# Expert rows folded over features before they are stored, and a Fourier stage that folds over tokens only

## The chip, the cores and the metric

The kernel runs on one core of a Trainium2 chip. A core has five engines that run side by side: TensorE (PE, matrix multiplication), VectorE (DVE), ScalarE (ACT), GpSimd (POOL) and SyncE (SP), the last of which here only issues transfers. TensorE reads its operands from SBUF, the on-chip memory of 128 partitions, and writes to PSUM, from where VectorE and ScalarE take the results. Sixteen DMA engines move data between SBUF and the chip's main memory (DRAM in the names). The metric is the device time of one execution in microseconds (us).

## The reference

Three layers follow each other on arrays of 4 batches, 576 tokens and 512 features: attention that keeps the 32 largest scores of a row, a layer of eight experts in which each token goes to one expert, and a mixing layer. The change concerns the last two.

```python
# experts: e is the token's expert, p[e] its weight
h = np.maximum(x[b, s] @ w1[e], 0.0)
out[b, s] = p[e] * (h @ w2[e])
...
# mixing
X = np.fft.fft(x, axis=1)          # over 576 tokens
X = np.fft.fft(X, axis=2)          # over 512 features
mixed = np.real(X).astype(np.float32)
u = x + mixed
un = (u - mean) / np.sqrt(var + 1e-06)   # over features
ch = np.maximum(un @ w_ch1, 0.0) @ w_ch2
return (u + ch).astype(np.float32)
```

## The kernel before

A Fourier transform over n points is done with matrix products. Its real part needs, of a row, only the sums x[d] + x[512 - d] (which meet cosines) and the differences x[d] - x[512 - d] (which meet sines), and likewise over tokens s and 576 - s. Making these sums and differences is called folding here, and it halves the length of the products. All products are made of pairs of shorter numbers, a high part (names ending in h) and a low part (l) with value = high + low, in three matmuls: high by high, high by low, low by high.

**Expert stage** (lines 1066 to 1263). Tokens were sorted by expert, and expert r of 8 works on up to CAPS[r] = 512 to 256 rows. It goes through f = 0 to 7, one step each: `mm1` makes 128 hidden features (PSUM tile `m`), ScalarE and VectorE turn them into `hh` and `hl`, and `mm2`, two steps later, adds their share to the output of up to four tiles of 128 rows. Between them stand the splits of the next expert's weights (`whi`, `wlo`) and the preparation of its rows (`xh`, `xl`). After f = 7, `finish(r)` copies the output tiles from PSUM to `ysb` with the factor p, and `store(r)`, called in step f = 2 of the next expert, or at the end for the last, scatters each tile of `ysb` with an indirect transfer from GpSimd's queue (`to_rows`) to the array `xm_d` in DRAM. A batch has 2 x 289 rows there: first tokens 1 to 288 and 0, then tokens 575, 574, ... down to 289, so that a row and the one 289 rows on are the pair that is folded over tokens.

**Fourier stage** (lines 1325 to 1477), for b = 0 to 3. `load_x(b)` reads the two halves to `xa` and `xb` in pieces of 112, 112 and 65 rows. `fold` adds and subtracts them over tokens (`fe` on VectorE, `fo` on GpSimd) and then folds each over features (256 to 511 onto 256 to 1). `parts` makes the high and low parts `eh`, `el` (258 columns) and `oh`, `ol` (256 columns). `over_tokens(b, c)`, c = 0 to 4, has nine matmuls for each of five chunks of features, three for `eh` and two for `oh`; ScalarE and VectorE take each from PSUM as high and low parts `ch`, `cl` or `sh`, `sl`. `over_features(b, j)`, j = 0 to 2, has nine matmuls into `pc` and six into `pn`; ScalarE copies `pc` to `cs`, VectorE makes the difference and the sum with `pn` (`dd`), which are stored to `md_d`. Batch b + 1 is folded while batch b is multiplied; batch 0 has its own order in `first()`.

**Norm and mixing.** `norm(g)` takes 256 rows of the sum of `xm_d` (tile `ut`) and `md_d` (`md`): GpSimd adds them, VectorE makes the statistics (`bs`, `mv`), ScalarE the deviation (`sd`), VectorE the scaled rows (written to `md`), and TensorE transposes them (`lt`), from where `nxh` and `nxl` are taken. The first two groups are normalized in the last batch of the Fourier stage, by the list `nops`; the others in the mixing that follows, which is bound by its matmuls (`f`).

Every engine works through its own instructions in the order in which the code emits them; nothing is reordered at run time. SyncE's transfers are issued in order too, and one that waits holds back those behind it.

## Time and profile before

| | |
|---|---|
| median of 3 runs | 1267.19 us (1265.48 to 1268.96) |
| the profiled execution, its own time | 1266.99 us |
| its span, from the first to the last instruction | 1264.8 us |
| TensorE busy | 1194.6 us, 94% of the span |
| VectorE busy | 866.9 us, 69% |
| ScalarE busy | 676.3 us, 53% |
| GpSimd busy | 446.0 us, 35% |

A row of the profile names an engine, a line of the code, an operation, the tile that it writes and those that it reads, and a shape (partitions x elements). PEld is TensorE's loading of weights, which overlaps its matmuls (PE). An engine may start an instruction shortly before the one ahead of it ends. The granted clock of TensorE is given as a share of 2.4 GHz: 1.00 is that level and 0.50 the other, 1.2 GHz, and what lies between is a mean over a stretch at both.

### The profile page before, as it was taken

The page shows a single profiled execution, that of the slowest core. Times are in us where ns is not written, and L with a number is a line of the kernel's source. Part 1 is how long each engine was busy: PE and PEld are TensorE (multiplying, and loading weights), DVE is VectorE, ACT ScalarE, POOL GpSimd, SP SyncE. Part 2 cuts the span into 40 slices and gives each one's busy share as a digit, 9 for nine tenths or more (in the row PEclk, how much of TensorE's full clock was granted, in tenths as well). Part 3 has the DMA queues.
Part 4 walks back from the last instruction along what each step waited for, and adds up shares of the span by engine and source line. Part 5 has one row for each costly group of instructions (what it writes and reads, how often), then busy time and mean ns, then how long its engine had stood idle before and what let it go on. Part 6 is the DMA issues. An engine that isn't in the chain of part 4 may idle for free. (4 is left out here: it accounts for less than half of the span.)

```text
span 1264.8 us, 25173 instructions
## 1 busy us (share of the span) xinstructions
PE 1194.6 (94%) x8691; PEld 1086.4 (86%) x8691; DVE 866.9 (69%) x3559; ACT 676.3 (53%) x1426; POOL 446.0 (35%) x553
## 2 busy tenths in 40 slices
PE   6999999999998995999999995979999999999997
PEld 5999889998998994898888885869999999999996
DVE  7999999999998985475666665847744444443222
ACT  6999999999997992354444542323322222221110
POOL 3767776786875683011111102713200000000122
PEclk9999999999998998999999995989999999999998
DMA  5757634443451413876666756632310010100111
GB/s 113 193 149 199 143 86 116 115 103 86 124 131 44 138 49 109 259 270 216 213 228 218 231 174 191 194 115 80 102 67 34 34 67 20 49 1 1 50 51 51
DMA packets 125653, 152.25 MB, mean 120 GB/s; under 512 B 68175, under 2 KB 70471, under 8 KB 125402
## 3 DMA queue, kind: packets, MB, share of 16 engines
q1 hardware_dynamic: 120442, 133.34, 36.8%
q0 software_dynamic: 5072, 17.19, 3.8%
q8 instruction: 71, 1.16, 0.4%
q14 instruction: 68, 0.56, 0.1%
HBM read 92.05 MB, written 32.79 MB: 99 GB/s over the span
## 5 line engine op out<-in xcount | busy, mean ns | idle before, releaser
L474 POOL TENSOR_TENSOR y<-ss,g 128x576 f32<-128x576 f32 x144 | 185.3, 1287 | 116.2 <-ACT g L469 58.3
L448 DVE MAX8 cd<-ss 128x8 f32<-128x72 f32 x1152 | 218.2, 220 | 10.0 <-ACT ss L442 9.5
L1529 ACT ACTIVATE fhh<-f 128x256 fp32r<-128x256 f32 x144 | 55.1, 383 | 278.9 <-PE f L1525 274.4
L1530 DVE SCALAR_TENSOR_TENSOR fhl<-f,fhh 128x256 fp32r<-128x256 f32 x144 | 60.9, 423 | 205.9 <-ACT fhh L1529 205.8
L545 PE MATMUL u<-in_v,et 128*128 128x74 f32 (+1 forms) x1600 | 185.5, 265 | 4.9 <-DVE dv L704 2.5
L545 PEld LDWEIGHTS u<-in_v,et 128*128 128x128 f32 (+1 forms) x1600 | 177.5, 181 | 10.0 <-ACT st_x L552 4.0
L528 PE MATMUL tp<-ident,z 128*128 128x128 f32 x720 | 142.6, 284 | 4.8 <-DVE lo L355 4.6
L529 PE MATMUL tp<-huge_id,bb 128*128 128x128 bf16 x720 | 131.7, 220 | 0.3 <-ACT bb L507 0.3
L435 PE MATMUL acc<-kt,qp 128*128 128x288 f32 x640 | 125.2, 323 | 6.3 <-ACT ss L442 4.0
L1550 POOL DMA_INDIRECT out_dram<-ut,orow x18 | 17.5, 971 | 319.4 <-DVE ut L1546 317.5
L469 ACT ACTIVATE g<-ss,mt 128x576 bf16<-128x576 f32 x144 | 118.0, 819 | 5.4 <-DVE mt L462 5.2
L528 PEld LDWEIGHTS tp<-ident,z 128*128 128x128 f32 x720 | 106.4, 148 | 15.6 <-POOL z L516 3.4
L507 ACT ACTIVATE bb<-ss,kth 128x576 bf16<-128x576 f32 x144 | 117.1, 813 | 0.0
L479 DVE MAX8 y<-y 128x8 f32<-128x576 f32 x144 | 107.0, 743 | 5.6 <-POOL y L474 5.6
L516 POOL TENSOR_SCALAR z<-ss,mt 128x576 f32<-128x576 f32 x144 | 107.8, 749 | 5.2 <-PE tp L529 5.2
L534 ACT ACTIVATE et<-tp 128x640 f32<-128x640 f32 x144 | 106.6, 740 | 2.4 <-PE tp L529 1.9
L442 ACT ACTIVATE ss<-acc 128x576 f32<-128x576 f32 x144 | 99.8, 693 | 11.6 <-PE acc L435 8.5
L941 POOL DMA_INDIRECT xm_d<-ysb,sid x23 | 24.6, 1068 | 228.8 <-ACT ysb L1187 225.1
L435 PEld LDWEIGHTS acc<-kt,qp 128*128 128x128 f32 x640 | 94.1, 197 | 9.7 <-ACT ss L442 5.0
L1525 PEld LDWEIGHTS f<-nxh,whi 128*128 128x128 f32 x576 | 87.8, 188 | 14.2 <-issue 1.2
L215 DVE TENSOR_TENSOR wlo<-raw,whi 128x1024 fp32r<-128x1024 f32 x70 | 85.5, 1260 | 14.8 <-ACT whi L214 14.4
L1541 PE MATMUL f<-whi,fhh 128*128 128x512 f32 x288 | 91.6, 399 | 0.7 <-ACT fhh L1529 0.7
(283 smaller groups left out, 2778.9 us busy)
## 6 DMA issues: line engine op xcount, KB each, us to landing
raw<-in_moe_w_dram SPq DMA_DIRECT2D x32, 1024.0 KB
kt<-hi SPq DMA_DIRECT2D x60, 144.0 KB
kt<-lo SPq DMA_DIRECT2D x60, 144.0 KB
xs_d<-xtok SPq DMA_DIRECT2D x8, 1056.0 KB
fr<-in_moe_w_ch_dram SPq DMA_DIRECT2D x16, 512.0 KB
raw<-in_moe_w_ch_dram SPq DMA_DIRECT2D x16, 512.0 KB
md<-md_d SPq DMA_DIRECT2D x9, 516.0 KB
in_k<-in_k_dram SPq DMA_DIRECT2D x32, 128.0 KB
```

What stands on the lines that cost most here:

```text
L435: PE.matmul(p, QP[i][:, s, o:o + 128].bitcast(F32R), KT[i][j][:, s, c].bitcast(F32R), start=(s == heads[0] and j == 0), stop=(s == heads[- ...
L442: ACT.activation(t.rearrange("p (h c) -> p h c", h=2), spb, AF.Copy)
L448: return [lambda j=j: DVE.max(cd[:, 8 * j:8 * j + 8], SS[n][:, 72 * j:72 * j + 72]) for j in range(8)]
L469: ACT.activation(g, SS[n], AF.Sign, bias=MT[i][:, t, 1, 7:8], scale=-SCL, accum_out=DIF[n])
L474: POOL.tensor_tensor(y, SS[n], LT[n], op=OP.mult)
L479: DVE.max(y8, Y8[n])
L507: ACT.activation(t, SS[n], AF.Relu, bias=kth[:, n:n + 1], scale=-1.0)
L516: POOL.tensor_scalar(ZZ[n], SS[n], -1.0, MT[i][:, t, 0, 0:1], op0=OP.mult, op1=OP.add)
L528: PE.matmul(o, z[:, k], ident, start=True, stop=False, is_transpose=True)
L529: PE.matmul(o, bb[:, k], huge_id, start=False, stop=True)
L534: ACT.activation(et, TP.pop(n).rearrange("p (c n) -> p c n", c=5), AF.Exp, scale=-1.0)
L545: PE.matmul(p[0:m, s, 0:VW], et[:, kc, qs], vv[:, kc, VC[s]], start=(kc == 0), stop=(kc == 4))
```

## The change

Each tile of expert output is folded over features by VectorE as soon as it is stored, and the folded tile goes to a second array `xf_d`, row for row like `xm_d`: sums of features d and 512 - d in columns 0 to 256, differences in columns 257 to 511. The folded tile is built in `xe`, a tile that the expert stage has no other use for by then. `store` runs in two steps (f = 2 and f = 4), two tiles each. The Fourier stage loads `xf_d` and folds over tokens only: VectorE adds columns 0 to 256 of `xb` to `xa` and subtracts the others, in place. The 289 rows are cut into three thirds of 96, with 97 partitions used, instead of 112, 112 and 65. GpSimd has no part in it. `eh`, `el`, `oh` and `ol` have two buffers, and are made at other places of the loop; the statistics of the two normalized groups start one batch earlier. A cosine table has a factor 0.5 at feature 256, which is now added to itself.

```diff
-    ts = np.zeros((112, 3, 4, 290), np.float32)
+    ts = np.zeros((KT_, 3, 4, 290), np.float32)
...
+    xf_d = dram.tile([B * 2 * NS, DM], F32, name="xf_d")
...
+    def fold_features(o, y):
+
+        DVE.tensor_tensor(o[:, 0:NE], y[:, 0:NE], y[:, 512:255:-1], op=OP.add)
+        DVE.tensor_tensor(o[:, NE:DM], y[:, 1:256], y[:, 511:256:-1], op=OP.subtract)
...
-                if c % 2:
-                    DVE.tensor_scalar(ysb[0:m, c], YP[r][c][0:m], pv[c][0:m], None, op0=OP.mult)
+                if c % 2 and r + 1 < E:
+                    DVE.tensor_scalar(ysb[0:m, c, 0:DM], YP[r][c][0:m], pv[c][0:m], None, op0=OP.mult)
...
+            for c, m in cs:
+                fold_features(xe[0:m, c % 2], ysb[0:m, c])
+                send(0, c, m)
+            for c, m in cs:
+                send(1, c, m)
...
-            if f == 2 and r > 0:
-                store(r - 1)
+            if f in (2, 4) and r > 0:
+                store(r - 1, (f - 2, f - 1))
...
-        store(E - 1)
+        store(E - 1, (0, 1))
...
-            for g, t in enumerate(XA[b]):
-                SP.dma_start(t[:, 0:2], x[g, 0:224].rearrange("(j p) d -> p j d", p=112))
-                SP.dma_start(t[0:63, 2], x[g, 224:287])
-
-            for t in XA[b]:
-                SP.dma_start(t[63:65, 2], x[0, 287:289])
...
+            SP.dma_start(xa[0:96], x[0, 0:288].rearrange("(j p) d -> p j d", p=96))
+            SP.dma_start(xb[0:96, 0:2], x[1, 0:192].rearrange("(j p) d -> p j d", p=96))
+            SP.dma_start(xb[0:95, 2], x[1, 192:287])
+            SP.dma_start(xa[96:97], x[0:1, 96:289:96])
+            SP.dma_start(xb[96:97, 0:2], x[1:2, 96:193:96])
+            SP.dma_start(xb[95:97, 2], x[0, 287:289])
...
-            DVE.tensor_tensor(t, xa, xb, op=OP.add)
-            POOL.tensor_tensor(u, xa, xb, op=OP.subtract)
-            DVE.tensor_tensor(t[:, :, 1:256], t[:, :, 1:256], t[:, :, 511:256:-1], op=OP.add)
-            POOL.tensor_tensor(u[:, :, 1:256], u[:, :, 1:256], u[:, :, 511:256:-1], op=OP.subtract)
...
+            c, _, op = COLS[i]
+            DVE.tensor_tensor(xa[:, j, c], xa[:, j, c], xb[:, j, c], op=op)
...
-                m = DT[j]
                 for x, y in ((hi, i), (hi, i + 1), (lo, i)):
-                    PE.matmul(p[0:dm], x[0:m, j, d0:d0 + dm], tst[0:m, j, y, :], start=(n == 0), stop=(n == 8))
+                    PE.matmul(p[0:dm], x[:, j, d0:d0 + dm], tst[:, j, y, :], start=(n == 0), stop=(n == 8))
...
+        for key, g, k in ((("F", 2, 0), 0, 1), (("F", 2, 1), 0, 2), (("F", 2, 1), 0, 3), (("F", 2, 2), 0, 4),
+                          (("T", 3, 0), 0, 5), (("T", 3, 2), 0, 6), (("T", 3, 1), 1, 1), (("T", 3, 2), 1, 2),
+                          (("T", 3, 3), 1, 3), (("T", 3, 4), 1, 4), (("F", 3, 0), 1, 5), (("F", 3, 2), 1, 6)):
+            at(key, g, k)
...
             for c in range(5):
                 over_tokens(b, c)
-                if more and c == 1:
-                    fold(b + 1, 0)
...
+                if more and c in (1, 2):
+                    fold(b + 1, c - 1)
+                    if c == 2:
+                        high(b + 1, 0)
+                        high(b + 1, 1)
+                if more and c in (3, 4):
+                    low(b + 1, c - 3)
```

In the list, ("T", b, c) is the place after `over_tokens(b, c)`, ("F", b, j) that after `over_features(b, j)`; the number behind it is the group, and the last the step: 1 and 3 statistics of its two halves, 2 and 4 their scaling, 5 and 6 its transposes.

Three places show how instructions move. The first is the end of the expert stage, on GpSimd's queue: the last expert's two scatters, the one ahead of them, and SyncE's first load of the Fourier stage as the last row. A scatter uses one of eight counters (DMASW0 to DMASW7) in turn, and waits for that counter's earlier use. Before:

```order
L941 DMA xm_d<-ysb,sid 2312x512 [waits DMASW4_49,DVE_49]
L1201 MEMSET spacer 1x1 [waits Pool_49]
L941 DMA xm_d<-ysb,sid 2312x512 [waits DMASW5_49,Activation_49]
L941 DMA xm_d<-ysb,sid 2312x512 [waits DMASW6_49,DVE_49]
L1338 DMA xa<-xm_d 112x2x512 [waits DMASW5_49,DMASW6_49,DMASW4_49,DMASW7_49,DMASW3_49,DMAHW1_49,DMASW2_49,DMAHW2_49,DMASW1_49,DMAHW5_49,DMASW0_49,DMAHW6_49,DVE_49,Pool_49]
```

and the same place of the change, from the last expert's first scatter on:

```order
L950 DMA xf_d<-xe,sid 2312x512 [waits DMASW3_49,DVE_49]
L1215 MEMSET spacer 1x1 [waits Pool_49]
L950 DMA xf_d<-xe,sid 2312x512 [waits DMASW4_49,DVE_49]
L950 DMA xm_d<-ysb,sid 2312x512 [waits DMASW5_49,Activation_49]
L950 DMA xm_d<-ysb,sid 2312x512 [waits DMASW6_49,Activation_49]
L1366 DMA xa<-xf_d 96x3x512 [waits DMASW4_49,DMASW5_49,DMASW3_49,DMASW6_49,DMASW2_49,DMASW7_49,DMASW1_49,DMAHW1_49,DMASW0_49,DMAHW2_49,DVE_49,DMAHW5_49,PE_49,DMAHW6_49,Activation_49,Pool_49]
```

Two scatters became four, and the first load names the counters of the last two, DMASW5 and DMASW6, which the scatters of `xm_d` raise; the count that it waits for is the one after them. 

The second place is VectorE in the batches b = 0 to 2, from the second chunk of a batch's tokens to its first `dd`. Before:

```order
L1386 TENSOR_TENSOR cl<-p_19970,ch 86x290
L1351 TENSOR_TENSOR fe<-xa,xb 112x1024
L1353 TENSOR_TENSOR fe<-fe 112x2x255
L1386 TENSOR_TENSOR cl<-p_19988,ch 86x290
L1386 TENSOR_TENSOR sl<-p_20000,sh 128x290
L1386 TENSOR_TENSOR sl<-p_20012,sh 128x290
L1408 TENSOR_TENSOR dd<-cs,pn 112x258
L1409 TENSOR_TENSOR dd<-cs,pn 112x258
L1365 TENSOR_TENSOR el<-fe,eh 112x516
```

and with the change:

```order
L1408 TENSOR_TENSOR cl<-p_20096,ch 86x290
L1382 TENSOR_TENSOR xa<-xa,xb 97x3x257
L1408 TENSOR_TENSOR cl<-p_20109,ch 86x290
L1382 TENSOR_TENSOR xa<-xa,xb 97x3x255
L1408 TENSOR_TENSOR sl<-p_20124,sh 128x290
L1389 TENSOR_TENSOR el<-xa,eh 97x774
L1408 TENSOR_TENSOR sl<-p_20137,sh 128x290
L1389 TENSOR_TENSOR ol<-xa,oh 97x768
L1430 TENSOR_TENSOR dd<-cs,pn 112x258
```

Both folds and both low parts now stand among the five chunks, an `el` ahead of the second `sl`. 

The third place is VectorE from the last `dd` of batch 2 on, into batch 3, where the first group is normalized. Before:

```order
L1408 TENSOR_TENSOR dd<-cs,pn 65x258
L1409 TENSOR_TENSOR dd<-cs,pn 65x258
L1386 TENSOR_TENSOR cl<-p_20308,ch 86x290
L1304 BN_STATS bs<-ut_20125 128x6
L1306 BN_AGGR mv<-bs 128x2
L1310 RECIPROCAL rs<-sd 128x1
L1311 TENSOR_SCALAR md<-ut_20125,mv,rs 128x512
L1386 TENSOR_TENSOR cl<-p_20329,ch 86x290
```

and with the change, from the first `dd` of batch 2:

```order
L1430 TENSOR_TENSOR dd<-cs,pn 112x258
L1431 TENSOR_TENSOR dd<-cs,pn 112x258
L1326 BN_STATS bs<-ut_20225 128x6
L1328 BN_AGGR mv<-bs 128x2
L1430 TENSOR_TENSOR dd<-cs,pn 112x258
L1431 TENSOR_TENSOR dd<-cs,pn 112x258
L1336 RECIPROCAL rs<-sd 128x1
L1337 TENSOR_SCALAR md<-ut_20225,mv,rs 128x512
L1326 BN_STATS bs<-ut_20225 128x6
L1328 BN_AGGR mv<-bs 128x2
L1430 TENSOR_TENSOR dd<-cs,pn 65x258
L1431 TENSOR_TENSOR dd<-cs,pn 65x258
```

The first group's two chains of statistics left the chunks of batch 3 and stand between the `dd` of batch 2; the four transposes of each half are emitted after chunks 0 and 2 of batch 3, and those of the second group after its features j = 0 and j = 2.

## Rows read from the trace of the kernel before

**Rows 1.** Waits of PE, 760 to 848 us: total us, times, longest.
```profile
PE p L1383 <- ACT eh L1429: 13.0, 1, 13.0
PE lt L1317 <- DVE md L1311: 6.3, 3, 3.0
...
PE f L1525 <- DVE dd L1409: 1.0, 1, 1.0
```

**Rows 2.** Busy time by stretch: PE, PEld, DVE, ACT, POOL, clock, DMA share, GB/s.
```profile
552.00:760.00 208.00, 207.54 (x1173) 181.45 (x1171) 133.72 (x214) 100.29 (x158) 23.94 (x42) 1.00 0.66 216
760.00:772.64 12.64, 0.00 (x1) 0.01 (x1) 2.47 (x5) 0.83 (x2) 2.09 (x4) 0.64 0.38 121
772.64:792.92 20.28, 19.75 (x90) 18.64 (x91) 17.65 (x27) 5.35 (x13) 8.46 (x5) 0.55 0.81 245
792.92:804.82 11.90, 11.86 (x93) 11.47 (x91) 10.11 (x18) 4.71 (x12) 7.77 (x5) 1.00 0.67 185
804.82:818.02 13.20, 12.43 (x92) 11.43 (x91) 11.13 (x18) 4.76 (x12) 9.41 (x7) 1.00 0.68 201
818.02:844.85 26.83, 18.22 (x108) 16.24 (x107) 16.52 (x37) 8.99 (x21) 6.96 (x7) 0.81 0.29 93
```

**Rows 3.** The chain that ended last, 860 to 866 us: start, us, what.
```profile
863.50 0.44 PE lt L1317 x4
```

**Rows 4.** Instructions in order of time, 759 to 779 us: start, us, what, idle before.
```profile
759.72 0.69 ACT L1187 ACTIVATE ysb<-acc,pv 128x512 f32<-128x512 f32 x1 [3.82 <-PE acc L1175]
...
760.69 0.98 POOL L941 DMA_INDIRECT xm_d<-ysb,sid  x1 [17.54 <-ACT ysb L1187]
...
761.98 0.99 POOL L941 DMA_INDIRECT xm_d<-ysb,sid  x1 [0.24 <-issue]
...
764.90 0.32 SPq L1338 DMA_DIRECT2D xa<-xm_d  x1
...
770.86 0.69 DVE L1427 TENSOR_TENSOR fe<-xa,xb 112x512 f32<-112x512 f32 x1 [9.65 <-DMA xb<-xm_d]
...
771.58 0.42 DVE L1428 TENSOR_TENSOR fe<-fe 112x255 f32<-112x255 f32 x1
...
772.64 0.78 PE L1383 MATMUL p<-tst,eh 112*86 112x290 f32 x2 [12.95 <-ACT eh L1429]
...
776.03 0.69 PE L1383 MATMUL p<-tst,eh 112*86 112x290 f32 x2
...
778.21 0.69 PE L1383 MATMUL p<-tst,eh 112*86 112x290 f32 x2
```

**Rows 5.** Instructions of DVE in order of time, sixth expert, around 721 us.
```profile
720.91 0.42 DVE L1156 SCALAR_TENSOR_TENSOR hl<-m,hh 128x256 fp32r<-128x256 f32 x1 [1.80 <-ACT hh L1155]
```

**Rows 6.** Busy time by stretch, columns as in rows 2, the first load.
```profile
767.00:768.00 1.00, 0.00 (x0) 0.00 (x0) 0.00 (x0) 0.00 (x0) 0.00 (x0) 0.50 1.08 361
...
770.00:771.00 1.00, 0.00 (x0) 0.00 (x0) 0.14 (x1) 0.00 (x0) 0.00 (x0) 0.50 0.29 96
```

**Rows 7.** Instructions in order of time, second and third batch, one engine each.
```profile
799.09 0.42 PE L1397 MATMUL pc<-tct,ch 86*112 86x258 f32 x2
...
802.14 0.69 DVE L1365 TENSOR_TENSOR el<-fe,eh 112x516 fp32r<-112x516 f32 x1
802.86 1.66 DVE L1351 TENSOR_TENSOR fe<-xa,xb 65x512 f32<-65x512 f32 x1
...
814.22 0.62 ACT L1363 ACTIVATE eh<-fe 112x516 fp32r<-112x516 f32 x1
```

**Rows 8.** Instructions in order of time, fourth batch, PE and DVE.
```profile
825.92 0.48 PE L1317 MATMUL lt<-ident,md 128*128 128x128 f32 x1 [3.02 <-DVE md L1311]
...
826.16 0.68 DVE L1304 BATCH_NORM_STATS2 bs<-ut 128x6 f32<-128x512 f32 x1
...
827.61 0.55 DVE L1311 TENSOR_SCALAR md<-ut,mv,rs 128x512 f32<-128x512 f32 x1
828.21 0.90 PE L1317 MATMUL lt<-ident,md 128*128 128x128 f32 x3 [1.81 <-DVE md L1311]
```

More of the change, by code (lines that the diff above doesn't have):

```diff
@@ L36 @@
 DT0 = (0, 112, 224)
+KT_ = 97
+NE = 257
 EC = (86, 86, 85)
@@ L1024, in overflow @@
                     PE.matmul(p, ho[:, f], wb[:, f], start=(f == 0), stop=(f == 7))
-                yo = op.tile([128, DM], F32, name="yo")
-                ACT.activation(yo, p, AF.Copy, scale=xo[:, DM:DM + 1])
-                to_rows(ix, yo)
+                yo = op.tile([128, DM + 1], F32, name="yo")
+                DVE.memset(yo[:, DM:DM + 1], 0.0)
+                ACT.activation(yo[:, 0:DM], p, AF.Copy, scale=xo[:, DM:DM + 1])
+                yf = op.tile([128, DM], F32, name="yf")
+                fold_features(yf, yo)
+                to_rows(ix, yf, xf_d)
+                to_rows(ix, yo[:, 0:DM], xm_d)
     slow = nc.values_load(slow_i[0:1, 0:1], min_val=0, max_val=1)
@@ L1320, in tr, with both @@
             DVE.tensor_tensor(xl[:, 2 * dd:2 * dd + 2], p, xh[:, 2 * dd:2 * dd + 2].bitcast(F32), op=OP.subtract)
-        return [add, lambda: ln(0), lambda: ln(1), lambda: tr(0), lambda: tr(1)]
+        def both(c):
+            stats(c)
+            scale(c)
+        if apart:
+            return [add, lambda: stats(0), lambda: scale(0), lambda: stats(1), lambda: scale(1), lambda: tr(0), lambda: tr(1)]
+        return [add, lambda: both(0), lambda: both(1), lambda: tr(0), lambda: tr(1)]
     with ExitStack() as ph:
@@ new lines, in load_x, with halves @@
+            x = xf_d[2 * b * NS:(2 * b + 2) * NS].rearrange("(g n) d -> g n d", g=2)
+            SP.dma_start(xa[0:96], x[0, 0:288].rearrange("(j p) d -> p j d", p=96))
[4 more added lines that the diff above has]
+            SP.dma_start(xb[95:97, 2], x[0, 287:289])
+        def halves(b):
+            EO[b] = [fp.tile([KT_, 3, n], F32R, name=nm, bufs=2)
+                     for nm, n in (("eh", 258), ("el", 258), ("oh", 256), ("ol", 256))]
@@ new lines, in body, with fold, high, low @@
+        COLS = ((slice(0, NE), slice(0, 258), OP.add), (slice(NE, DM), slice(256, DM), OP.subtract))
+        def fold(b, i, j=slice(0, 3)):
+            xa, xb = XA[b]
+            c, _, op = COLS[i]
+            DVE.tensor_tensor(xa[:, j, c], xa[:, j, c], xb[:, j, c], op=op)
+        def high(b, i, j=slice(0, 3)):
+            ACT.activation(EO[b][2 * i][:, j], XA[b][0][:, j, COLS[i][1]], AF.Copy)
+        def low(b, i, j=slice(0, 3)):
+            hi, lo = EO[b][2 * i:2 * i + 2]
+            DVE.tensor_tensor(lo[:, j], XA[b][0][:, j, COLS[i][1]], hi[:, j].bitcast(F32), op=OP.subtract)
@@ L1431, in low @@
-            def low(j, i):
-                m, n = DT[j], (258, 256)[i]
-                DVE.tensor_tensor((el, ol)[i][0:m, j], fs[i][0:m, j % 2, 0:n], (eh, oh)[i][0:m, j].bitcast(F32), op=OP.subtract)
-            for i in range(2):
-                add(0, i)
-                if i == 0:
-                    SP.dma_start(fp.tile([1, 1], F32, name="after", bufs=1), fs[0][0:1, 0, 0:1])
-                    load_x(1)
-                add(1, i)
-                low(0, i)
-                add(2, i)
-                low(1, i)
-                low(2, i)
+            halves(0)
@@ new lines, in first @@
+            js = [slice(j, j + 1) for j in range(3)]
+            fold(0, 0, js[0])
+            fold(0, 1, js[0])
+            high(0, 0, js[0])
+            SP.dma_start(fp.tile([1, 1], F32, name="after", bufs=1), XA[0][0][0:1, 0, 0:1])
+            load_x(1)
+            for j in (1, 2):
+                fold(0, 0, js[j])
+                fold(0, 1, js[j])
+                high(0, 0, js[j])
+                low(0, 0, js[j - 1])
+            high(0, 1)
+            low(0, 0, js[2])
+            low(0, 1)
@@ L1466, in body @@
+                for o in nops.pop(("T", b, c), ()):
+                    o()
             if b == 0:
@@ L1470, in body @@
                 over_features(b, j)
-                if more and j == 0:
-                    parts(b + 1, 0)
-                    fold(b + 1, 1)
-                    parts(b + 1, 1)
-                if b >= B - 2 and j == 2 or b == B - 1 and j < 2:
-                    for o in nops.pop(0) if nops else ():
-                        o()
+                for o in nops.pop(("F", b, j), ()):
+                    o()
+        assert not nops
     tables.close()
```

104 lines of the change are left out of this document (40 added, 64 removed).

## The prediction

> **What bounds the kernel now.** I read the waits of TensorE first, then the busy time of each engine batch by batch, then the instructions around the largest wait. Over the Fourier stage the waits list two large items [rows 1]: 13.0 us, once, before the first Fourier matmul, and 6.3 us in three pieces before the transposes of the normalized rows. The others are small. The table of stretches [rows 2] says the same in busy time: in the expert stage TensorE is busy 207.54 of 208 us, so there only TensorE's own work counts; between the stages it stands for 12.64 us; the first batch takes 20.28 us at a clock of 0.55, which is nearly all at the lower of the two levels (1.2 GHz); the second takes 11.90 us without a gap; the third 13.20; and the fourth 26.83, of which TensorE is busy 18.22.
>
> Four batches do the same matmuls, and the change keeps their number and their moving columns (45 over tokens, 45 over features). What can move is therefore the hole before the Fourier stage, and what the third and fourth batch have above 11.9 us. The fourth also holds 16 transposes; four take 0.44 us at the full clock [rows 3], so its work is 11.9 + 4 x 0.44 = 13.7 us. Its 26.83 us are then 13.7 of work, 18.22 - 13.7 = 4.5 from the low clock, and 8.6 of standing. That 13.1 us is the most that the fourth batch can give; the third has 1.3.
>
> **The expert stage.** Each of 23 tiles of expert output gains two VectorE instructions (257 and 255 columns) and a second scatter. A fold of 255 columns takes 0.42 us [rows 4], so a tile costs 0.84, and all of them 19 us. VectorE has 208 - 133.72 = 74 us free there [rows 2]. What matters is whether an hl (the low part of the hidden layer, which TensorE reads) comes late. The folds of two tiles (1.68 us) stand behind the hl of step 2; in the sixth expert VectorE then idles for 1.80 us before the next hl [rows 5], so they fit; the later tiles stand behind a pair of weight splits, and TensorE needs an hl only two steps on. The second scatters run on GpSimd and its DMA queue, which nothing on TensorE's path uses until the last expert. I take 0; the bound above is the slow rival's.
>
> **The hole before the Fourier stage.** Today [rows 4]: ysb is copied at 759.72, the two last scatters start at 760.69 and 761.98, the first load is issued at 764.90 (2.92 us after the last scatter began), the first addition starts at 770.86, and TensorE at 772.64. After the change the last expert's queue on GpSimd is four scatters, two of xf_d and two of xm_d, and the first load waits for all four: the order of its waits names the counters of the xm_d scatters too, as its tile takes over space of the expert stage, from which they still read. So the load moves by
> - +0.8: the first scatter now waits for both folds of its tile (2 x 0.42) after the copy;
> - +2.6: two more scatters at 761.98 - 760.69 = 1.29 each.
>
> The load itself brings the same 1.18 MB, but the first fold now needs five of its six transfers instead of the first and third: 577 rows of 2 KB instead of 511 (112 + 112 + 63 + 112 + 112). The missing 135 KB cost 0.4 us at the best rate of the load, 361 GB/s, and 1.4 at that of its last microsecond, 96 [rows 6]. They come last, so I take **+1.2**. The Trainium skill (DMA: Bandwidth & Descriptors, "Why a DMA increments its semaphore by 16 and not by 1") says a transfer uses the largest number of engines up to 16 that divides its rows: 95 rows would go to five engines. By that rule these carry 51 rows against 35 today; as an estimate, at 361 GB/s over 16 engines, that is +1.45, and the sum would be 0.25 higher. The falling rate in rows 6 agrees with some engines ending late.
>
> Then the first fold no longer has a 512-column addition (0.69) ahead of a 255-column one: from the first fold to the matmul it took 1.78 us, and now two instructions of 0.42 and a copy of the same size, 1.3: **-0.5**. The first chunk of nine matmuls took 3.4 us, from 772.64 to 776.03, and the next, without a wait, 2.2 [rows 4]; the order of the folds by thirds brings each low part sooner, and I count 2.6: **-0.8**. The rest of the first batch runs at the low clock as before. Sum at the start: 3.4 + 1.2 - 0.5 - 0.8 = **+3.3 us**.
>
> **Second and third batch.** GpSimd's share (a subtraction, a fold, a low part) is gone, and with it the late eh that holds the third batch. VectorE now has four instructions of about 770 columns: 0.42 for 255 and 0.69 for 516 [rows 4, 7] make 0.96 each; beside GpSimd's subtraction 512 columns took 1.66 [rows 7], and that company is gone. But their place is new. In the second batch the chunks of matmuls end at 1.28, 2.48, 3.7, 4.95 and 6.17 us (features start at 799.09, 6.17 after the batch began [rows 7]). ScalarE has ch of chunk 3 at 4.1, then eh and oh of all three thirds (0.62 for 516 columns [rows 7], so about 0.85 each), each behind its fold on VectorE (3.35 to 4.25, and 4.6 to 5.5): oh ends at 6.35, the first sh at 6.7, its sl at 7.2. Then el (0.96) stands ahead of the second sl, which ends at 8.4. TensorE reaches the matmul that needs it at 6.17 + 1.1 + 0.6 = 7.85. So a wait of **0.6** in each: second batch 11.9 to 12.5, third 13.2 to 12.5. Together -0.1. Bounds: -1.3 without that wait, +1 if the loads come later.
>
> **Fourth batch.** The statistics of the first group move into the third batch's features. Count from the start of these features. The low parts end at 8.4 + 0.9 - 6.2 = 3.2 us. Then VectorE has, in order, three pairs of dd (258 columns each, 0.8 a pair), and two chains of statistics to scaled rows, which took 2.0 us from 826.16 to the end of the row of 827.61 [rows 8]; twice a pair waits for ScalarE's cs behind sd (0.4 each): 3.2 + 2.4 + 4.0 + 0.8 = 10.4. TensorE gets to the transposes after the features (5.7 + 0.6) and one chunk (1.3), at 7.6. It waits 2.8 us, and more if the sums on GpSimd, which need their loads first, are late: **3.0**, where the group waited 3.02 + 1.81 today [rows 8]. The second group's statistics stand among the sl of the last chunks: by the same count the second sh waits behind sd for 0.9, and the first transposes 0.5: **1.4**. The last four transposes move behind the last features, into the 1.0 us which TensorE waits for dd there [rows 1]: 0.55 is left. Standing: 3.0 + 1.4 + 0.6 = 5.0 against 8.6. The low clock cost 4.5 behind gaps of 3.02, 1.81 and (the rest of the 6.3) 1.5 us; with one long gap left I take 2.0. So 13.7 + 5.0 + 2.0 = 20.7 against 26.8: **-6.1 us**; -10 with no wait above a microsecond and the full clock, -4 with both at today's size.
>
> **The sum**: 3.3 - 0.1 - 6.1 = -2.9 us. The profiled execution took 1266.99 us (span 1264.8), 0.2 below the median of 1267.19, so the forecast is **1264 us**.
>
> **Rivals.**
> - *The statistics do not hold TensorE at all* (the chain starts earlier than I count, the sl wait is absent too). For it: VectorE does less in a batch than today. Against: dd, sd and cs wait for one another in a fixed order. -10 in the fourth batch, -1 before: 1258 to 1260 us. Chance 0.22.
> - *The clock comes back sooner in the first batch.* After the hole it stayed low for 18 us (0.9 of 20.28, at a mean of 0.55), while the 4.5 us lost in the fourth batch mean 9 us at 1.2 GHz, over three gaps. With 3 to 9 us at the low level the first batch would be 4.5 to 7.5 us shorter: 1257 to 1260 us. Nothing in the change asks for it, but the hole and the matmuls' rows shift. Chance 0.10.
> - *Slower: the folds hold hl in the expert stage.* The place is the step after a pair of splits, where a tile's 0.84 us comes on top. It decides from the point at which an hl ends after the matmuls two steps on should begin, since these need its PSUM buffer. If half of the 0.84 us of the 21 tiles that fold within the stage reaches TensorE, that is 9 us: 1273 us, and 1267 to 1273 for less. Against: TensorE waits nowhere there today, and VectorE keeps a quarter of the time free. Chance 0.10.
> - *The load does not wait for the two xm_d scatters* (the change does what its order of scatters suggests): 2.6 less, 1261 us. The waits in the program speak against it. Chance 0.05.
>
> **How the numbers follow.** My forecast has 0.53, with a range of its own of 1261 to 1268: the start at 2.5 to 4.9, the fourth batch at -8 to -4, the middle at -0.7 to 0.7. Runs of this kernel agree within 0.3% (3.8 us), which is what a measurement can tell from no change; faster then means below 1263.2, slower above 1270.8. Of my own 0.53, 0.13 lies below 1263.2 and 0.02 above 1270.8; the rivals add 0.37 below and, of the slow one, 0.08 above and 0.02 between: 0.50 faster, 0.40 same, 0.10 slower. The range 1258 to 1270 takes in the first rival and most of the fourth, and leaves out the clock and the slow case.
>
> **What will show it.** First load about 3.4 us later after the experts' last copy, with four scatters ahead; first matmul 16 to 17 us after that copy, against 12.9 (759.72 to 772.64); a wait on sl of about 0.6 us in the second and third batch; a wait on md of 2.5 to 4 us before the first transposes, and a fourth batch near 21 us; TensorE without waits in the expert stage. I am wrong if the hole does not grow, if the fourth batch stays above 24 us or falls below 17, or if hl shows up among TensorE's waits.

## The result, and the profile after

The change makes the kernel slower: median 1274.84 us (1273.02 to 1275.95, 5 runs) against 1265.67 us (1265.45 to 1268.96, 5 runs) before, a ratio of 1.0062 (95% interval 1.0046 to 1.0078). The forecast was 1264, faster or the same; it missed in size and in sign.

The profiled execution of the changed kernel took 1275.95 us with a span of 1274.2. Cut at the starts of TensorE's own matmuls (the first of each stage and batch, the last of the experts and of the mixing), the spans of the two profiled executions compare as follows, in us:

| stretch | before | after | change | forecast |
|---|---|---|---|---|
| up to the experts' first matmul | 506.90 | 508.82 | +1.9 | 0 |
| expert stage | 252.4 | 254.9 | +2.5 | 0 |
| hole before the Fourier stage | 13.35 | 18.85 | +5.5 | +4.1 |
| first batch | 20.3 | 21.4 | +1.1 | -0.8 |
| second and third batch | 25.1 | 27.7 | +2.6 | -0.1 |
| fourth batch | 26.8 | 20.0 | -6.8 | -6.1 |
| mixing, to its last matmul | 410.3 | 410.9 | +0.6 | 0 |
| behind the last matmul | 9.7 | 11.5 | +1.9 | 0 |

The busy time by stretch of the changed kernel, columns as in [rows 2], from the expert stage to the fourth batch:

```profile
508.82:763.72 254.90, 252.20 (x1445) 222.29 (x1446) 173.03 (x301) 119.50 (x190) 51.81 (x87) 0.99 0.74 241
763.72:782.57 18.85, 0.40 (x3) 0.00 (x1) 2.88 (x10) 1.69 (x3) 4.44 (x8) 0.64 0.36 100
782.57:803.96 21.39, 18.41 (x91) 17.02 (x91) 9.85 (x20) 6.03 (x13) 0.00 (x0) 0.68 0.86 241
803.96:818.57 14.61, 13.69 (x92) 13.02 (x91) 7.75 (x15) 4.46 (x10) 0.00 (x0) 0.88 0.56 151
818.57:831.70 13.13, 12.20 (x92) 11.54 (x91) 8.87 (x15) 5.06 (x10) 4.11 (x3) 1.00 0.72 227
831.70:851.70 20.00, 16.04 (x109) 14.70 (x107) 12.69 (x32) 6.75 (x18) 1.24 (x2) 0.91 0.31 93
```

GpSimd does nothing in the first two batches, as meant, and VectorE has only 9.85 us of work in the first batch, against 17.65 in [rows 2]. Yet TensorE stands for 3 us of it. The waits of TensorE from 764 to 853 us, in the columns of [rows 1], name who it waits for:

```profile
PE p L1405 <- ACT eh L1385: 18.5, 1, 18.5
PE lt L1343 <- DVE md L1337: 3.3, 3, 2.5
PE pn L1425 <- ACT sh L1407: 3.0, 3, 2.4
PE pn L1425 <- DVE sl L1408: 1.5, 3, 0.6
...
```

In the kernel before, sl and sh held TensorE once each, and for less; these are the last two lines of the list that [rows 1] is taken from:

```profile
PE pn L1403 <- DVE sl L1386: 0.4, 1, 0.4
PE pn L1403 <- ACT sh L1385: 0.3, 1, 0.3
```

Three stretches of the first batch show the clock: it comes back 6.8 us into the batch, against 18.1 before (772.64 to 790.73), and falls again for 6.8 us behind the wait of 2.4 us on sh.

```profile
782.57:789.30 6.73, 6.73 (x27) 6.25 (x28) 3.67 (x9) 2.39 (x5) 0.00 (x0) 0.50 0.91 205
789.30:796.10 6.80, 4.07 (x30) 3.65 (x28) 2.22 (x4) 2.35 (x5) 0.00 (x0) 0.99 0.82 227
796.10:803.00 6.90, 6.65 (x29) 6.16 (x30) 3.96 (x8) 0.91 (x3) 0.00 (x0) 0.51 0.86 297
```

The hole, in order of time, beside [rows 4]:

```profile
764.15 1.27 ACT L1199 ACTIVATE ysb<-acc,pv 128x512 f32<-128x512 f32 x2 [3.81 <-PE acc L1188]
...
765.91 1.24 POOL L950 DMA_INDIRECT xf_d<-xe,sid  x1 [12.50 <-DVE xe L947]
...
770.02 0.98 POOL L950 DMA_INDIRECT xm_d<-ysb,sid  x1 [0.24 <-issue]
...
772.93 0.32 SPq L1366 DMA_DIRECT2D xa<-xf_d  x1
...
781.18 1.43 DVE L1382 TENSOR_TENSOR xa<-xa,xb 97x257 f32<-97x257 f32 x4 [10.99 <-DMA xb<-xf_d]
...
782.57 0.78 PE L1405 MATMUL p<-tst,eh 97*86 97x290 f32 x2 [18.45 <-ACT eh L1385]
```

The steps of the forecast can be read off: the first scatter 0.79 later after the copy (1.76 against 0.97; forecast 0.8), the last 4.11 after the first instead of 1.29 (+2.8; forecast 2.6), the load again 2.91 behind the last, the first matmul 1.39 behind the first fold instead of 1.78 (-0.4; forecast -0.5). The load is off: 8.25 us from its first issue to the first fold against 5.96, so +2.3 where +1.2 was forecast.

In the expert stage three waits of TensorE are left, two of them new, 2.1 us together:

```profile
PE m L1164 <- ACT xh L1120: 2.3, 2, 1.6
PE acc L1188 <- DVE ysb L1197: 1.3, 1, 1.3
PE m L1164 <- DVE xl L1127: 0.8, 1, 0.8
```

The wait on xl comes just behind this place, shown in order of time on GpSimd and VectorE; the one on ysb ends 8 us later (745.50):

```profile
732.26 1.06 POOL L950 DMA_INDIRECT xm_d<-ysb,sid  x1 [0.22 <-ACT hh L1168]
...
737.19 0.16 DVE L262 SCALAR_TENSOR_TENSOR sid<-xsl,em 128x2 int32<-128x2 f32 x1 [4.14 <-DMA xm_d<-ysb,sid]
737.27 0.41 DVE L1127 TENSOR_TENSOR xl<-tp,xh 128x256 fp32r<-128x256 f32 x1
```

VectorE stands for 4.14 us because it is to write the next expert's row numbers (`sid`, two buffers) over those that the scatters of the second step (f = 4) still read. Six such waits make 9.3 us in the stage; before there was none. The kernel before issues all scatters in step 2.

### The profile page after: what moved, and what is told of

The parts are those of the page before. It is cut to its first block, busy times and chain, and to the rows that moved or that the text cites. A ratio compares the mean times of both kernels' runs of the same rounds, so it can differ in the third digit from the quotient of the medians.

```text
span 1274.2 us, 25273 instructions
## 1 busy us (share of the span) xinstructions
PE 1194.8 (94%) x8691; PEld 1087.3 (85%) x8691; DVE 865.0 (68%) x3590; ACT 675.2 (53%) x1419; POOL 450.0 (35%) x582
## 5 line engine op out<-in xcount | busy, mean ns | idle before, releaser
L446 ACT ACTIVATE ss<-acc 128x576 f32<-128x576 f32 x144 | 100.0, 694 | 12.5 <-PE acc L439 8.7
L950 POOL DMA_INDIRECT xf_d<-xe,sid x23 | 25.8, 1122 | 200.6 <-DVE xe L947 198.5
```

## The experiments

The theory then had five parts: (1) the buffer of sid holds VectorE in the expert stage; (2) all four scatters stand ahead of the load; (3) the load is slow because of how it is cut; (4) the high and low parts of the next batch stand ahead of sh and sl, and what TensorE waits there costs twice, by the wait and by a low clock after it; (5) the earlier statistics give the fourth batch its gain. The main rivals: the folds' own time on VectorE, the competition of loads, and GpSimd's freedom. Each edit below is against the changed kernel. A single profiled execution took between 503.8 and 509.5 us up to the experts, in code that no edit touches, so parts are compared by stretch, and totals only where several executions were timed.

**sid with three buffers** (e1).

```
-            sid = mp.tile([128, XCAP // 128, 1], I32, name="sid", bufs=2)
+            sid = mp.tile([128, XCAP // 128, 1], I32, name="sid", bufs=3)
```

> The changed kernel with a third buffer for the row numbers (sid). Theory: the expert stage lost its 2.5 us because VectorE, before it writes the next expert's sid, now waits for the scatters of the second step, which still read that buffer (9.3 us of such waits, the longest 4.14 us, behind which xl and the last expert's work are late). Then the waits on sid go, the expert stage falls from 255.3 to about 252.8 us, and the median by about 2.5 us, from 1274.8 to 1272.3. Rival: the folds' own 19 us on VectorE, or the second scatters, hold the stage. Then it stays at 255 us and the waits of TensorE on ysb and xl stay.

Measured: 1271.12 us (8 runs), ratio 1.0041 (1.0023 to 1.0059). The expert stage, by stretch, is 1.8 us shorter, and TensorE's waits on ysb and xl are gone, with all folds in place:

```profile
506.22:759.31 253.09, 252.25 (x1446) 222.87 (x1446) 173.51 (x301) 119.88 (x190) 51.69 (x87) 0.99 0.74 243
```

Part 1 holds. The 173.5 us of VectorE's work do not hold TensorE.

**The load of batch 2 emitted later** (e2), and **the same load made to wait** (e5).

```
         first()
-        load_x(2)
...
             if b == 0:
+                load_x(2)                                  # e2
...
                     fold(b + 1, c - 1)
+                    if b == 0 and c == 1:                  # e5
+                        SP.dma_start(fp.tile([1, 1], F32, name="after", bufs=1), XA[1][0][0:1, 0, 0:1])
+                        load_x(2)
```

> The changed kernel with the load of batch 2 issued behind the five chunks of batch 0, as before the change. Theory: the load of batch 1 lands 9.6 us after its first issue because the load of batch 2, issued 3.5 us behind it, shares the DMA engines; its late folds then hold sh for 2.40 us in the first batch, and the clock falls again behind that. Then batch 1's data land about 3 us sooner, the wait on sh is below 0.8 us, the clock stays at its upper level to the end of the batch, and the first batch falls from 21.4 us to 16 to 17: median about 1270. Rival: the load of batch 1 takes 9 us by itself (its small transfers, the scattered engines). Then the first batch stays at 21 us and the median at 1274.

> The changed kernel in which the load of batch 2 really waits: a 4-byte transfer that reads the folded data of batch 1 stands ahead of it on SyncE. (In the run with the later place SyncE's own order was the same, so it issued that load at the same moment, and nothing moved.) Theory: the two loads share the DMA engines, so the load of batch 1 lands 2 to 3 us sooner than 9.6 us after its first issue, the wait of 2.40 us on sh in the first batch falls below 0.8, and that batch from 21.4 to 16 to 19 us. Rival: the load of batch 1 is slow by itself. Then its folds start at the same time and the first batch stays at 21 us.

Measured: e2 1273.44 us, ratio 1.0064 (1.0043 to 1.0084); it tells nothing, since SyncE has no other instruction between the two places and issued the load when it did before. e5: 1271.63 us, ratio 1.0050 (1.0035 to 1.0065). Its first batch took 21.04 us, and the two waits on sh and sl in it are these:

```profile
794.88 0.50 PE L1425 MATMUL pn<-tnt,sh 128*112 128x258 f32 x2 [1.93 <-ACT sh L1407]
796.62 0.56 PE L1425 MATMUL pn<-tnt,sl 128*112 128x258 f32 x1 [0.62 <-DVE sl L1408]
```

The folds of batch 1 began 8.74 us after the load's first issue (781.99 to 790.73), against 9.63 (782.31 to 791.94) in the changed kernel, and 9.55 to 9.84 in the seven executions that leave this load and its folds as they are. So competition costs about 0.9 us, not 2 to 3: the rival is nearer.

**The old places of the normalization** (e3).

```
-        for key, g, k in ((("F", 2, 0), 0, 1), (("F", 2, 1), 0, 2), (("F", 2, 1), 0, 3), (("F", 2, 2), 0, 4),
...
+        for key, g, k in ((("F", 2, 2), 0, 0), (("T", 3, 0), 0, 1), (("T", 3, 1), 0, 2), (("T", 3, 2), 0, 3), (("T", 3, 2), 1, 0),
+                          (("T", 3, 3), 0, 4), (("T", 3, 3), 1, 1), (("T", 3, 4), 1, 2), (("F", 3, 0), 1, 3), (("F", 3, 1), 1, 4)):
```

> The changed kernel with the normalization of the two groups placed as before the change (sums behind the third batch's last features, both statistics within the fourth batch). Theory: the earlier statistics give the 6.8 us of the fourth batch. Then that batch goes back to 25 to 27 us, the third falls by at most 0.3, and the median rises by 5 to 6 us to about 1280. Rival: it is GpSimd's freedom that gives it, since its sums can now start 2 to 3 us sooner. Then the fourth batch takes 20 to 23 us and the median is 1275 to 1277.

Measured: 1275.22 us, ratio 1.0077 (1.0057 to 1.0098). Part 5 falls: with the old places the fourth batch takes 20.83 us. GpSimd's first sum, in order of time:

```profile
822.67 1.28 POOL L1319 TENSOR_TENSOR ut<-ut,md 128x514 f32<-128x514 f32 x1 [56.64 <-DMA ut<-xm_d]
```

and the batch, by stretch:

```profile
826.34:847.17 20.83, 15.74 (x109) 14.58 (x107) 13.68 (x33) 7.60 (x17) 1.31 (x2) 0.92 0.26 77
```

The sums start 3.7 us ahead of the batch. In the kernel before they started 2.95 us into it, behind the last low part that GpSimd made for the batch, a share that it no longer has. But they were not what held the first statistics: VectorE stood only 0.43 us for them. It came to the first statistics 5.3 us into the batch (823.34 from 818.02), as the last fold, the last low part and two pairs of dd still stood ahead there; in e3 it comes to them 2.2 us into the batch (828.55 from 826.34) and waits for nothing. Two rows from before, then one of e3:

```profile
820.97 1.30 POOL L1299 TENSOR_TENSOR ut<-ut,md 128x514 f32<-128x514 f32 x1
823.34 0.69 DVE L1304 BATCH_NORM_STATS2 bs<-ut 128x6 f32<-128x512 f32 x1 [0.43 <-POOL ut L1300]
...
828.55 0.68 DVE L1326 BATCH_NORM_STATS2 bs<-ut 128x6 f32<-128x512 f32 x1
```

So 6.0 of the 6.8 us come without the new places; by these rows, mainly from the folds and low parts that VectorE and GpSimd no longer have there. How much each engine's share gives was not run apart. The 0.8 us that is left to the new places is no more than this batch varies: in the nine executions that leave it as the change has it, it takes 18.6 to 21.0 us.

**Two scatters less at the end** (e4).

```
+            if f == 5 and r + 1 == E:
+                send(r, 1, 0, 128)
+                send(r, 1, 1, CAPS[r] - 128)
...
-            for c, m in cs:
-                send(1, c, m)
+            if r + 1 < E:
+                for c, m in cs:
+                    send(r, 1, c, m)
```

> The changed kernel in which the last expert's two scatters to the unfolded array run in that expert's step 5, where they carry rows of the expert before (so these rows of the sum are not the reference's), and not at its end. Theory of the prediction: the first load of the Fourier stage waits for all scatters of the expert stage, so with two less at the end it is issued 2.6 us sooner, and the hole falls from 18.85 us (TensorE's last matmul of the experts to its first of the Fourier stage) to 16.2: median lower by 2.6. Rival: the load is held by something else, or the shorter hole is given back in the first batch. Then the hole falls by less than 1 us, or the first batch grows by 1 us or more.

Measured: 1271.03 us, ratio 1.0048 (1.0030 to 1.0065). Part 2 holds: the hole is 2.87 us shorter (the load itself took 0.3 less in this execution), and the first batch with 21.0 us gives nothing back:

```profile
758.67:774.65 15.98, 0.39 (x3) 0.01 (x1) 2.89 (x10) 1.68 (x3) 2.36 (x4) 0.66 0.34 96
```

**Another order of folds, high and low parts** (e6).

```
+        steps = {(True, "T", 0): [(fold, 0)], (True, "T", 1): [(fold, 1), (high, 0)], (True, "T", 2): [(high, 1), (low, 0)],
+                 (True, "T", 4): [(low, 1)], (False, "T", 4): [(fold, 0), (fold, 1)],
+                 (False, "F", 0): [(high, 0), (high, 1), (low, 0)], (False, "F", 1): [(low, 1)]}
...
-                if more and c in (1, 2):
-                    fold(b + 1, c - 1)
...
+                for o, i in steps.get((b > 0, "T", c), ()) if more else ():
+                    o(b + 1, i)
```

> The changed kernel with another order of the next batch's folds, high and low parts: in the first batch behind its last chunk (folds) and among its features (high and low parts); in the second and third the folds behind chunks 0 and 1, the high parts behind chunks 1 and 2, the low parts behind chunks 2 and 4. Theory: the waits on sh and sl (2.40 and 0.25 in the first batch, 0.30 and 0.63 in the second and third) come from high and low parts that stand ahead of sh and sl on ScalarE and VectorE, and the clock that falls to its lower level a little later is their second price. Then these waits go, the first batch takes 15 to 17 us instead of 21.4, the second and third 12 to 12.5 each, and the median falls by 7 to 9 us to about 1266. Rival: the clock falls in any case some 15 us after the hole, or the next batch's eh comes late instead. Then the first two batches together lose less than 3 us.

Measured: 1266.81 us (10 runs), ratio 1.0003 (0.9988 to 1.0018). This edit alone takes the loss back. The four batches by stretch:

```profile
777.68:791.95 14.27, 14.27 (x90) 13.79 (x91) 9.07 (x19) 5.87 (x12) 0.00 (x0) 0.79 0.87 217
791.95:803.50 11.55, 11.55 (x92) 11.47 (x91) 8.53 (x17) 4.84 (x11) 0.00 (x0) 1.00 0.97 293
803.50:816.91 13.41, 12.58 (x92) 11.62 (x91) 7.00 (x13) 4.85 (x9) 0.60 (x1) 1.00 0.92 287
816.91:840.10 23.19, 16.22 (x109) 14.77 (x107) 13.55 (x34) 6.70 (x18) 4.06 (x4) 0.85 0.26 80
```

Part 4 holds: in the first two batches TensorE stands nowhere, and the clock stays at its upper level once it is back. They take 7.1 and 3.1 us less than in the changed kernel, where the waits were only 3.0 and 0.9; the third, which has new waits of 0.5 and 0.2 us on cl and sl, gains nothing (13.41 against 13.13). In the fourth batch 3.2 us are lost again: the earlier batches end sooner, the sums' loads stay behind SyncE's other transfers, VectorE stands 4.12 us for GpSimd's sum, and md now comes too late (6.0 us of TensorE's waits):

```profile
818.69 0.69 DVE L1326 BATCH_NORM_STATS2 bs<-ut 128x6 f32<-128x512 f32 x1 [4.12 <-POOL ut L1320]
```

**More scatters** (e7).

```
+                if r + 1 < E:
+                    send(2, c, m)          # to xg_d, which nothing reads
```

> The changed kernel with a third scatter of each tile but the last expert's, to an array that nothing reads (21 more). It asks where the 1.9 us behind the last matmul went, which all profiles of the changed kernel have more than the kernel before (11.5 against 9.7): GpSimd's last instruction there, the drain of its queue at the end of the program, takes 8.4 us instead of 6.6. Theory: the drain's length follows the number of scatters that GpSimd issued in the whole program (23 more gave 1.87 us, so 0.081 each). Then it takes 1.7 us longer still, 10.1, and the tail is 13.2 us. Rival: it follows the program's size or the last scatters alone: tail within 0.3 of 11.5.

Measured: 1279.06 us in one run; 13.25 us behind the start of the last matmul. The last row of GpSimd before the change (span 1264.8 us):

```profile
1258.58 0.09 POOL L1556 MEMSET spacer<- 1x1 f32 x1
```

in the changed kernel (span 1274.2 us):

```profile
1266.01 0.09 POOL L1578 MEMSET spacer<- 1x1 f32 x1
```

and with 21 more scatters (span 1277.3 us):

```profile
1267.41 0.09 POOL L1581 MEMSET spacer<- 1x1 f32 x1
```

The expert stage of that run, by stretch:

```profile
509.52:767.14 257.62, 253.62 (x1446) 222.92 (x1446) 172.49 (x301) 119.45 (x190) 74.54 (x129) 0.99 0.76 255
```

From the end of the last row of GpSimd the span goes on for 8.1 and 9.8 us; before the change it was 6.2. Twenty-three scatters more cost 1.9 and 21 more another 1.7: 0.08 us each, at the very end of the program, although all had landed 500 us earlier. The expert stage grew by 2.7 us too, as the extra scatters hold sid still longer (VectorE's six waits on it make 21.1 us): part 1 again.

**The load, cut otherwise** (e8) **and in another order** (e9), **and from the other array** (e12).

```
-            SP.dma_start(xb[0:95, 2], x[1, 192:287])        # e8
+            SP.dma_start(xb[0:80, 2], x[1, 192:272])
+            SP.dma_start(xb[80:95, 2], x[1, 272:287])
...
+            SP.dma_start(xa[96:97], x[0:1, 96:289:96])      # e9: these three ahead of the large ones
+            SP.dma_start(xb[96:97, 0:2], x[1:2, 96:193:96])
+            SP.dma_start(xb[95:97, 2], x[0, 287:289])
             SP.dma_start(xa[0:96], x[0, 0:288].rearrange("(j p) d -> p j d", p=96))
...
-            x = xf_d[2 * b * NS:(2 * b + 2) * NS]           # e12
+            x = (xf_d if b else xm_d)[2 * b * NS:(2 * b + 2) * NS]
```

> The changed kernel with the transfer of 95 rows in the load cut into one of 80 and one of 15. Theory: the load is late because the 95 rows go to few of the sixteen DMA engines (the rate falls from 352 to 131 and 25 GB/s while the last bytes come), so the time from its first issue to the first fold falls from 8.25 us to 6.7 to 7.2, and the hole by as much, from 18.85 to about 17.5. Rival: the small transfers behind it, issued up to 2.8 us late, set the end; with one more issue ahead of them the first fold comes 0.3 to 0.5 us later, not sooner.

> The changed kernel with the three small transfers of the load (rows of the 97th partition and the two unpaired rows) ahead of the three large ones. By the theory that the few engines of the 95 rows set the end, these bytes now start about 1.8 us later, and the first fold comes 1 to 2 us later. By the rival, that the late small transfers set it, the first fold comes 0.5 to 1.5 us sooner.

> The changed kernel whose first batch is loaded from the unfolded array with the same six transfers (so its transform is of other values). In the changed kernel's first load a packet of 2 KB takes 0.137 us in the mean, in the kernel before 0.109, and the first fold comes 8.25 us after the first issue. Theory: that is the cut of the transfers (96 rows of three thirds, single partitions). Then it stays at 0.13 to 0.14 and 8.0 to 8.3 us. Rival: it is the array, just written or placed elsewhere. Then it falls to 0.11 and the first fold comes about 1 us sooner.

Measured, from the first issue to the first fold: e8 7.80 us (1266.79 us in its one run), e9 8.28 (1273.58), e12 7.61 (1273.38), where the eight executions of this load as the change has it lie between 7.74 and 8.26. To the first fold the split is thus worth half a microsecond at most, and the order (e9) nothing in sum. The array is not the cause: from the unfolded one it is hardly faster, far from 5.96.

The counters that the transfers raise as they land, in the trace's records, say more. VectorE's first fold waits for four of the six transfers: the two large ones, landed 5.37 and 6.44 us after the first issue in the changed kernel, and the two pieces of the 97th partition, landed after 8.03 and 8.09. The 95 rows, for which this fold does not wait, are issued between them and land after 7.85. Before, the first fold waited for two transfers, landed after 3.62 and 5.83. So of the 2.3 us more, 0.6 are the large transfers and 1.7 the two pieces behind the 95 rows. These pieces land 1.5 to 1.9 us behind the large transfers in the nine executions whose 95 rows go whole and in this order, and 0.7 to 0.9 in the three with the split (e8, e10, e11): the 95 rows are about half of it. In e8 the last of the four has landed after 7.29 us; VectorE then still has four waits to pass, 0.1 us each, and the fold starts at 7.80. In e9 the two pieces have landed after 2.11 and 2.77 us, but the issues of the small transfers take SyncE 1.96 us, so the large ones come later, at 7.04 and 8.15: what one end gains the other loses. The order with the two pieces between the large transfers and the 95 rows was not run.

The load of batch 1 is cut in the same way, and its folds wait for all of it, so there split and order both show. These are e8's first issue of that load, the fold that waits for it, and the matmul that waits in the end:

```profile
778.46 0.37 SPq L1366 DMA_DIRECT2D xa<-xf_d  x1
...
786.28 0.96 DVE L1383 TENSOR_TENSOR xa<-xa,xb 97x771 f32<-97x771 f32 x1 [1.71 <-DMA xb<-xf_d]
...
790.45 0.49 PE L1426 MATMUL pn<-tnt,sh 128*112 128x258 f32 x2 [0.69 <-ACT sh L1408]
```

That is 7.82 us instead of 9.63; the wait on sh falls from 2.40 to 0.69 us, the clock does not fall again, and the first batch takes 17.28 us instead of 21.39:

```profile
778.72:796.00 17.28, 15.96 (x90) 14.81 (x91) 9.86 (x20) 6.03 (x13) 0.00 (x0) 0.77 0.97 270
```

In e9, where the 95 rows come last, the same fold starts 10.98 us after the first issue: the two large transfers have landed after 6.69 and 8.44 us, the 95 rows after 10.86.

```profile
779.73 0.69 SPq L1366 DMA_DIRECT2D xa<-xf_d  x1
...
790.71 0.96 DVE L1382 TENSOR_TENSOR xa<-xa,xb 97x771 f32<-97x771 f32 x1 [4.88 <-DMA xb<-xf_d]
```

By the rule of the Trainium skill (DMA: Bandwidth & Descriptors, "Why a DMA increments its semaphore by 16 and not by 1") 95 rows go to five engines and 80 rows to sixteen. The trace agrees: the counters rise by five landings for the 95 rows and by sixteen for the 80. This 1.8 us agrees with it too, while the first fold shows at most half a microsecond of the 1.45 that was worked out from it, and the landings of the pieces about 0.8.

**The changes mended** (e10), and **the statistics sooner** (e11). e10 joins e1, e6 and e8 with two more edits:

```
+            if b == 1:
+                for g in range(2):
+                    load_u(g, lp)           # was at the start of b == 2
...
+            if r + 1 == E:
+                for c, m in cs:
+                    send(1, c, m)           # ahead of the folds, for the last expert
```

and e11 moves the statistics of e10:

```
+        for key, g, k in ((("T", 2, 4), 0, 1), (("F", 2, 0), 0, 2), (("F", 2, 0), 0, 3), (("F", 2, 1), 0, 4),
+                          (("T", 3, 0), 0, 5), (("T", 3, 2), 0, 6), (("F", 2, 2), 1, 1), (("T", 3, 0), 1, 2),
+                          (("T", 3, 1), 1, 3), (("T", 3, 2), 1, 4), (("F", 3, 0), 1, 5), (("F", 3, 2), 1, 6)):
```

> The changed kernel with what the runs showed put right: a third buffer for sid; the order of folds, high and low parts of the run with that order; the two groups of the sum loaded behind the second batch's chunks, not ahead of the third; the last expert's scatters to the unfolded array ahead of its folds; the load with 80 and 15 rows. Theory: from that run's 1266.8, -1.8 in the expert stage, -0.9 from the folds hidden and -1.2 from the load in the hole, and in the third and fourth batch (13.4 and 23.2 there) -1 and -5, as GpSimd's sums are there when VectorE wants them: 1255 to 1258 us, a ratio to the kernel before of about 0.993. Rival: the clock falls elsewhere in the Fourier stage, or the earlier sums hold something new, and the gain there is given back: 1260 to 1264.

> The mended kernel with the statistics one place sooner: the first group's begin behind the third batch's last chunk and end among its features, the second group's begin behind these features. In the mended kernel the first transposes of the fourth batch wait 2.32 us for the scaled rows, and the clock falls behind that. Theory: VectorE waits for no sum of GpSimd there any more, so the wait on md falls below 0.6 us, the fourth batch from 20.1 to 16 to 17.5 us, the third stays at 12 to 12.5: median 1255 to 1257. Rival: the statistics now hold sl or dd in the third batch, and what the fourth gains the third loses: within 1 us of 1258.8.

Measured: e10 1258.84 us (6 runs), ratio to the kernel before 0.9951 (0.9933 to 0.9969); e11 1255.65 us (6 runs), ratio 0.9913 (0.9892 to 0.9934). Both beat both kernels; e10 missed its forecast by 0.8 us, as its fourth batch kept a wait of 2.3 us on md and a low clock behind it (20.1 us). e11 came out in its range, though its wait on md is 1.0 us (below 0.6 was forecast) and its third batch 12.71 (12 to 12.5). e11, from the expert stage to the fourth batch:

```profile
506.76:759.16 252.40, 251.57 (x1445) 222.09 (x1446) 173.54 (x301) 119.54 (x190) 51.67 (x87) 0.99 0.74 243
759.16:776.26 17.10, 0.41 (x3) 0.01 (x1) 2.89 (x10) 1.69 (x3) 4.24 (x8) 0.64 0.39 110
776.26:791.57 15.31, 15.31 (x91) 14.83 (x92) 9.08 (x19) 5.87 (x12) 0.00 (x0) 0.73 0.98 260
791.57:803.11 11.54, 11.54 (x92) 11.46 (x91) 8.53 (x17) 4.84 (x11) 0.00 (x0) 1.00 0.97 271
803.11:815.82 12.71, 11.89 (x93) 11.45 (x92) 9.70 (x18) 5.14 (x10) 6.13 (x4) 1.00 0.73 249
815.82:832.07 16.25, 14.08 (x108) 13.12 (x107) 11.52 (x30) 6.31 (x17) 0.00 (x0) 1.00 0.39 118
```

The expert stage is back at 252.4. The hole, 3.7 us longer than before the change, and the end of the program, 1.9 longer, are what the extra scatters and the cut of the load still cost.

## Why the prediction was wrong

By its own steps, against the change of the table above:

- **The expert stage, taken as 0: wrong (+2.5).** The step looked for who reads what the folds delay, found hl, and costed the second scatters at nothing because GpSimd is free. It never asked who writes again what the moved scatters read. e1 and e7 show that it is sid. The slow rival named the right stage and side, but by the folds' time, which e1 excludes.
- **The hole: the mechanism right, one term mis-sized.** The load's +1.2 measured +2.3 in the profiled execution (1.8 to 2.3 over eight of them, against the one execution before). The step took five of the six transfers as needed, 577 rows by its count (they have 580), and priced the rows that came on top by the rates at the end of the old load. By the counters the first fold needs four transfers, and 1.7 of the 2.3 us are its last two, five rows that stand behind the 95; about half of that goes with the 95 rows. The mean time of a 2 KB packet (counted over the trace's records of that load), 0.137 us instead of 0.109, does not set it: in e8 it is 0.140, and the last packet ends 1.0 us sooner.
- **First chunk -0.8: right** (2.5 us from 782.57 to the next chunk at 785.10). **"The rest of the first batch runs at the low clock as before": wrong.** The clock came back 6.8 us into the batch, as the second rival had it, and 5.9 to 8.2 us into it in all thirteen executions of the changed kernel and its variants; what brings it back sooner than the 18.1 us of the one execution before, no run shows. By the rival's count that is worth (18 - 6.8) / 2 = 5.6 us; the batch gave it back, since the forecast looked at the place of eh, oh, el and ol only from the second batch on. In the first the load of batch 1 comes late, the high parts stand on ScalarE ahead of sh for 2.40 us, and the clock then falls for another 6.8 us. e6 and e8 show both ends of that chain.
- **Second and third batch, -0.1: wrong (+2.6), though the forecast wait on sl came (0.62 us in each).** Another 0.30 on sh stands ahead of it, and behind the pair the clock fell for 3.4 us in one of the two batches, in four executions the second, in four others the third, and in e8 and e9 in neither. Without these waits (e6) the second batch takes 11.55 us; with them 13.1, and 14.6 where the clock falls. The step priced one wait at 0.6, where the pair costs 1.6, and not what the clock does behind it.
- **Fourth batch, -6.1 against -6.8: right in size, wrong in cause.** What is left was counted well: the longest wait on md is 2.5 us (3.0 forecast), all standing 4.0 (5.0). But the forecast credits the new places of the statistics, and with the old ones (e3) 6.0 of the 6.8 us are there all the same; the other 0.8 is within what this batch varies. The step left out what the folds taken from VectorE and GpSimd give here: even with the old places (e3) VectorE comes to the first statistics 3.1 us sooner. Of that, GpSimd's late sums had cost 0.43. That the size came out is thus in part luck. Nor were the new places run with the old shares of the two engines.
- **The end of the program, not in the sum: +1.9.** e7 shows that it follows the count of scatters.
- The rest of the profiled difference (1.9 us up to the experts, 0.6 in the mixing) lies within what these stretches vary from execution to execution.

## What to carry to other kernels

When a transfer is moved to a later step, look for the next writer of everything that it reads, indices too: with two buffers, that writer may stand at the head of the busiest queue. Work prepared for the next stage belongs behind the small evictions that TensorE waits for now, on every engine that does both; waits of 3.0 us there cost 7.1 us in the first batch, where the clock fell behind them, and waits of 0.9 us cost 1.6 in each of the next two, or 3.1 where it fell. And when an engine is freed and a schedule is moved in one change, test them apart before either is given the gain.

## What the runs showed of the hardware

- The end of the program waits longer the more indirect scatters GpSimd has issued in all: 6.2, 8.1 and 9.8 us behind its last instruction with 0, 23 and 44 more, 0.08 us each.
- The issue of a transfer of a single partition in three rows took SyncE 0.81 us in the first load, against 0.32 for one of 96 partitions in three rows; in the next load 0.68 against 0.37.
- A transfer of 95 rows landed in five parts, one of 80 rows in sixteen, one of 15 in fifteen. Issued last (e9), the 95 rows landed 1.2 us behind the larger transfer ahead of them in the first load and 2.4 in the second; in the changed kernel's first load, small pieces issued behind them landed 0.2 us after these.
- The waits ahead of one instruction are passed one after another: in e8 VectorE passed four, for transfers that had all landed, 0.1 us apart.
- The same pair of waits (0.30 and 0.62 us, 1.7 us apart) was followed by 3.4 us at the lower clock in one batch and by none in the next; which of the two differed between executions, and in two of ten neither was.
